# Cutting a weight load by partitions, and moving two cut points: attention decode with a parallel MLP on one core

## The chip, the core and the metric

The kernel runs on one core of one Trainium2 chip. A core has a matrix engine (PE), a vector engine (DVE), an activation engine (ACT), GpSimd (POOL) and a sync engine (SP), which here does nothing but issue transfers. Sixteen DMA engines move data between the memory outside the core (DRAM) and the on-chip memory (SBUF, 128 partitions). The metric is device time in microseconds (us) of one execution; lower is better. Before the change the median of three runs is 1283.76 us (1283.54 to 1283.78).

## The reference, cut to what matters

The batch is 8, with one query token of 640 values each. There are 32 heads of 128 values with 4096 cached keys and values, all in bfloat16. The block normalises x, runs attention over the caches and an MLP beside it, and adds both to x:

```
xn = layernorm(x)
q  = (xn @ wq), 32 heads of 128
o  = softmax(q k^T * 128^-0.5) v        # k, v: caches of 8 x 32 x 4096 x 128
out = x + o @ wo + (gelu(layernorm(xn) @ w1 + b1) @ w2 + b2)
```

The caches are 512 MB of the 552 MB that are read; wq and wo are 5.2 MB each, w1 and w2 2.2 MB each.

## The kernel before, in words

The work is cut into 32 items. Item i is one batch entry and one group of eight heads; its keys are one 8 MB load and its values another. A load fills one slot of the large tile `S_sb` with all 128 partitions: partition p holds 256 keys of one head (16 partitions for each head), 64 KB in one row. `S_sb` has three slots: two take the keys in turns, and the third takes the values, one item after another.

For each item, 176 of the 256 key columns are scored on DVE in three chunks (multiply, add, reduce), and 80 on PE and ACT (transposes, copies and small matmuls). Then come the maximum, the exponentials on ACT, and `pe_PV` (line 633): 256 matmuls, one for each key column, that accumulate the output of the item. The next value load may start only when `pe_PV` is done with the slot (`load_v`, line 362); the next key load waits until the item two before has been read (`load_k`, line 350).

Before the first item, the same slots hold the weights of the small stages: `wq_sb` and `w1_sb` lie in the value slot and `w2_sb` in a key slot. `wq_sb` has one row of 40 KB in each of 128 partitions (row p holds five of the 640 input rows). `w2` comes in two loads: `w2a` with 128 partitions, and `w2b`, the last 64 rows of w2, with 64 partitions. `pe_q` (line 448) waits for wq and makes all queries; `pe_mlp1` waits for w1, `pe_mlp2` for w2. The end of the MLP releases the second key slot and the value slot.

At the end, the key slot of item 30 takes wo in parts. `load_wl` brings two head groups and then one (`WL_CUT`), and `load_wn` brings the last group in three pieces (`WN_CUT`), each with a semaphore. `fin_wl` and `fin_wn` multiply them into the accumulator in the same order, and `fin_store` adds up and stores. The value load of the last item is cut into four pieces by key columns (`V_CUT`). The first of these may start when `pe_PV` of item 30 has gone through as many key columns as the piece has (the ticket `pvh`, set inside `pe_PV`); the other three wait for its end. `pe_PV` of the last item waits for each piece when it gets to its first column.

The order of work on each engine is written out by hand: `at(position, function, ...)` gives each step a place, the steps are sorted, and each engine replays its own list. All loads but the smallest are issued by SP, one after another, in this order: wq, w1, w2a, w2b, keys of item 0 in two pieces, and then keys and values by turns. The three small loads of x, b1 and b2 go out from ACT's queue.

Of the kernel before, what the change touches and what calls it, by code (L numbers as in the profile page):

```python
# [14 lines left out]
P = 128  # L15
# [176 lines left out]
def bass_parallel_sum__gqa_block_cached__mixer_channel_mlp__decode_kernel(  # L192
# [17 lines left out]
    HS = 8  # L210
# [4 lines left out]
    DC = D // P  # L215
# [7 lines left out]
    SLOT = NKEY * DH  # L223
    KA, KB, VS = 0, 1, 2
    WL_CUT = (0, 2, 3)
    WN_CUT = (0, 4, 7, HS)
    V_CUT = (0, 96, 176, 240, 256)
    K_CUT = (0, 117, 256)

    def jp_of(i):  # L230
# [17 lines left out]
    with ExitStack() as es:  # L248
# [3 lines left out]
        sem = lambda name: es.enter_context(nc.semaphore(name))  # L252
# [4 lines left out]
        def part(slot, lo, n, rows=P):  # L257
            return S_sb[0:rows, slot, lo:lo + n]

        wq_sb = part(VS, 0, DC * H * DH).rearrange("p (c n) -> p c n", c=DC)  # L260
# [6 lines left out]
        def scratch(n, rows=P):  # L267
# [60 lines left out]
        pe, dve, act, sp, pool = (_Eng(sem(f"{n}_s")) for n in ("pe", "dve", "act", "sp", "pool"))  # L328
        pe2, act2 = _Eng(sem("pe2_s")), _Eng(sem("act2_s"))
        ld_s = [_Dma(sem(f"ld_s{s}")) for s in range(3)]  # L330
        ld_x, ld_b1, ld_b2, ld_wq, ld_w1, ld_w2a, ld_w2b, st_o = (
            _Dma(sem(n)) for n in ("ld_x", "ld_b1", "ld_b2", "ld_wq", "ld_w1", "ld_w2a", "ld_w2b", "st_o"))
        ld_vl = [_Dma(sem(f"ld_vl{q}")) for q in range(1, len(V_CUT) - 1)]
        ld_k0 = _Dma(sem("ld_k0"))
        ld_wl = [_Dma(sem(f"ld_wl{q}")) for q in range(len(WL_CUT) - 1)]
        ld_wn = [_Dma(sem(f"ld_wn{q}")) for q in range(len(WN_CUT) - 1)]
        tk = {}
        prog = []

        def at(pos, fn, *a):  # L340
            prog.append((pos, len(prog), fn, a))
# [20 lines left out]
        def load_v(i):  # L362
# [4 lines left out]
            tk[("v", i)] = []  # L367
            for d, lo, hi in zip([ld_s[VS]] + ld_vl, V_CUT[:-1], V_CUT[1:]):
                if lo:
# [13 lines left out]
        def load_wn(q):  # L383
            lo, hi = WN_CUT[q], WN_CUT[q + 1]
            n = HS * DH
            tk[("wn", q)] = ld_wn[q].sig(sp.dma_start(
                woL_sb[:, NL, lo * D:hi * D],
                A_wo[NL * n:(NL + 1) * n, :].rearrange("(p s) n -> p (s n)", p=P)[:, lo * D:hi * D]))

        def consts_pool():  # L390
            pool.iota(iota_h, [[-HP, HS]], base=0, channel_multiplier=1)
            tk["iota"] = pool.sig(pool.iota(iota_i, [[1, P]], base=0, channel_multiplier=-1))
            for d, (ap, v) in zip([None] + ld_vl, (
                    (zeros_sb, 0.0), (ones_sb, 1.0), (mx_sb[:, :], 0.0), (mb_sb[:, :], 0.0))):
                inst = pool.memset(ap, v)
                if d is not None:
                    inst.call[3] = (d.sem, 1)
            tk["consts"] = pool.sig(pool.memset(ones_f[:, :], 1.0))
# [47 lines left out]
                xT_sb[:, w, :, :].rearrange("p c b -> p (c b)"), TR_ps[:, w, 0:DC * B])))  # L446

        def pe_q():
            pe.wait(tk["wq"], tk[("xT", 0)])
            CHB.use(pe)  # L450
            for h in range(H):
                for c in range(DC):
                    last = pe.matmul(QT_ps[:, h * B:(h + 1) * B], wq_sb[:, c, h * P:(h + 1) * P],
                                     xT_sb[:, 0, c, :], start=(c == 0), stop=(c == DC - 1))
            CHB.used(pe, pe.sig(last))
# [177 lines left out]
        def pe_PV(i):  # L633
            PVB.use(pe)
            pe.wait(tk[("exp", i)])
            for j in range(NKEY):
                if j == 0:
                    pe.wait(tk[("v", i)][0])
                elif j in V_CUT:
                    pe.wait_ge(ld_vl[V_CUT.index(j) - 1].sem, 1)  # L640
                last = pe.matmul(PV_ps[:, 0:HS], tile[VS][:, j, :], P_sb[:, :, j],
                                 start=(j == 0), stop=(j == NKEY - 1))
                if j == V_CUT[1] - 1:
                    tk[("pvh", i)] = pe2.sig(last)
# [86 lines left out]
        def fin_wn(q):  # L731
            lo, hi = WN_CUT[q], WN_CUT[q + 1]
            pe.wait(tk[("wn", q)], tk[("oS3", 0)], tk[("oS3", 1)])
            for r in range(lo, hi):
                for c in range(DC):
                    last = pe.matmul(ACC_ps[:, c * B:(c + 1) * B],
                                     woL_sb[:, NL, r * D + c * P:r * D + (c + 1) * P], oS3_sb[:, r, :],
                                     start=False, stop=(r == HS - 1), skip_group_check=True)
            if hi == HS:
                ACCB.used(pe, pe.sig(last))  # L740
# [16 lines left out]
        at(-900, load, "x", ld_x, x_sb, x2, act)  # L757
        at(-899, load, "b1", ld_b1, b1_sb, B_b1.rearrange("(o f) -> o f", o=1), act)
        at(-898, load, "b2", ld_b2, b2_sb, B_b2.rearrange("(o f) -> o f", o=1), act)
        at(-890, load, "wq", ld_wq, wq_sb, A_wq.rearrange("(p c) n -> p c n", c=DC))  # L760
        at(-880, load, "w1", ld_w1, w1_sb, B_w1.rearrange("(p c) f -> p c f", c=DC))
        at(-879, load, "w2a", ld_w2a, w2_sb[:, 0:FB, :], B_w2[0:FB * P, :].rearrange("(p c) n -> p c n", c=FB))
        at(-878, load, "w2b", ld_w2b, w2_sb[0:FLAST, FB, :], B_w2[FB * P:F, :])
        at(-870, load_k, 0)
        at(-800, consts_pool)
        at(-795, idents)
        at(NQ * Q - 1, sel_pool)
# [5 lines left out]
        at(-772, cp_xT, 1)  # L773
        at(-771, pe_acc0)
        at(-770, pe_q)
        at(-765, cp_q)
        at(-740, pe_mlp1)
# [35 lines left out]
        for q in range(len(WL_CUT) - 1):  # L813
            at(o - 55 if q == 0 else o + 50 + 0.1 * q, load_wl, q)
            at(o + 79.1 + 0.2 * q, fin_wl, q)
        for q in range(len(WN_CUT) - 1):
            at(o + 51 + q, load_wn, q)
# [80 lines left out]
```

## Time and profile before

The table is from one profiled execution.

| What | Value |
|---|---|
| median of three runs | 1283.76 us |
| profiled execution, its own time | 1283.81 us |
| its span, first to last instruction | 1281.8 us |
| moved by the main DMA queue | 551.79 MB, 11152 packets |
| mean rate over the span | 431 GB/s |
| busy share: DVE, PE, ACT, POOL | 85%, 52%, 37%, 7% |
| one item in the middle of the run | 38.7 us (7.0 us `pe_PV`, 31.6 us until the next values land) |
| wq: issue to landing | 15.7 us |
| pieces of the last group of wo: issue to landing | 21.6, 22.3 and 22.2 us |

To read it: the page cuts the span into 40 slices and gives for each the busy share of every engine in tenths, the mean share of the 16 DMA engines and the GB/s that they moved. Queries of the trace give the same for any stretch. In such a stretch a transfer's packet is counted where it starts, so a short stretch can show a share over 1; over a few microseconds it evens out. A packet here is one row of one partition, such as 64 KB for the caches and 40 KB for wq. The ratio of GB/s to share tells how fast the packets went that started there.

### The profile page before, as it was taken

The numbers are of one execution on the slowest core, as the hardware profiler recorded it, in microseconds if no ns is written. First come the engines' busy times: TensorE is split into PE (matmuls) and PEld (weight loads), VectorE is DVE, ScalarE is ACT, GpSimd is POOL, SyncE is SP. The second block draws the span as 40 slices with busy tenths as digits, with TensorE's granted clock in tenths as the row PEclk, the third lists the DMA queues.
The fourth block names the chain that finished last, engine by engine and source line by source line (L and its number), as shares of the span: only waits on it lengthen the run. The fifth ranks groups of instructions, "written<-read, shape, count | busy, mean of one in ns | idle before, by whom it ended". The sixth has DMA issues, their size and how long they took to land.

```text
span 1281.8 us, 34444 instructions
## 1 busy us (share of the span) xinstructions
PE 671.3 (52%) x13944; PEld 575.0 (45%) x13944; DVE 1095.1 (85%) x675; ACT 475.1 (37%) x904; POOL 88.7 (7%) x108
## 2 busy tenths in 40 slices
PE   4365554564544564544664644654545655545645
PEld 4254443453443553433553534543434544434545
DVE  1799988988888988888988888988889988889885
ACT  1344432344432344423344423344323344323441
POOL 0001000000000000000000000000000000000001
PEclk9955655566655656555655555565555555555555
DMA  9999999999999999999999999999999999999998
GB/s 396 436 439 424 442 427 438 427 442 427 436 429 442 427 436 429 442 427 434 432 442 427 434 432 440 429 434 432 440 430 432 432 442 429 432 432 442 429 417 369
DMA packets 11235, 551.99 MB, mean 431 GB/s; under 512 B 1292, under 2 KB 1493, under 8 KB 1878
## 3 DMA queue, kind: packets, MB, share of 16 engines
q1 hardware_dynamic: 11152, 551.79, 99.7%
q8 instruction: 9, 0.15, 0.0%
q10 hardware_dynamic: 70, 0.03, 0.0%
q14 instruction: 4, 0.03, 0.0%
HBM read 551.80 MB, written 0.01 MB: 430 GB/s over the span
## 4 chain that ended last, share of the span: by engine, by line
DMA 80%; PE 19%; ACT 1%; issue 1%; SPq 0%; another core or an unknown queue 0%; DVE 0%; POOL 0%; ACTq 0%
DMA S_sb<-in_A_v_cache_dram 74%; PE PV_ps L111 17%; DMA S_sb<-in_A_k_cache_dram 3%; DMA S_sb<-in_A_wo_dram 2%; DMA S_sb<-in_B_w_dram 2%; PE TR_ps L111 1%; PE CH_ps L111 1%; ACT P_sb L111 0%; PE ACC_ps L111 0%; SPq L111 0%; PE S_ps L111 0%; ACT KT_sb L111 0%; PE QB_ps L111 0%; ACT S_sb L111 0%
## 5 line engine op out<-in xcount | busy, mean ns | idle before, releaser
L111 PE MATMUL TR_ps<-ident_bf,S_sb 128*128 128x128 bf16 (+1 forms) x2570 | 341.5, 278 | 376.8 <-POOL kr_sb L111 366.0
L111 DVE TENSOR_TENSOR S_sb<-S_sb,qbc_sb 128x7552 bf16<-128x7552 bf16 (+1 forms) x96 | 388.8, 4050 | 136.8 <-DMA S_sb<-in_A_k_cache_dram 136.8
L111 PEld LDWEIGHTS TR_ps<-ident_bf,S_sb 128*128 (+2 forms) x2570 | 244.8, 103 | 434.6 <-issue 360.3
L111 DVE TENSOR_REDUCE Sd_sb<-S_sb 128x59 f32<-128x3776 bf16 (+1 forms) x96 | 390.2, 4065 | 6.0
L111 ACT ACTIVATE KT_sb<-TR_ps 128x1024 bf16<-128x1024 bf16 x320 | 326.9, 1023 | 125.6 <-PE TR_ps L111 115.5
L111 PE MATMUL PV_ps<-P_sb,S_sb 128*128 128x8 bf16 x8192 | 224.0, 175 | 149.3 <-DMA S_sb<-in_A_v_cache_dram 146.2
L111 PEld LDWEIGHTS PV_ps<-P_sb,S_sb 128*128 128x128 bf16 x8192 | 221.2, 103 | 152.2 <-DMA S_sb<-in_A_v_cache_dram 149.0
L111 ACT ACTIVATE P_sb<-Sd_sb,NB_sb 128x256 bf16<-128x256 f32 x256 | 126.2, 494 | 218.5 <-DVE NB_sb L111 218.5
L111 DVE TENSOR_TENSOR S_sb<-S_sb 128x3776 bf16<-128x3776 bf16 (+1 forms) x96 | 202.9, 2114 | 3.3
L111 ACT ACTIVATE oU_sb<-PV_ps 128x8 f32<-128x8 f32 x31 | 5.5, 177 | 393.2 <-PE PV_ps L111 393.2
L111 PE MATMUL S_ps<-qrep_sb,KT_sb 128*128 128x8 bf16 x2560 | 122.0, 177 | 35.5 <-ACT KT_sb L111 31.8
L111 PEld LDWEIGHTS S_ps<-qrep_sb,KT_sb 128*128 128x128 bf16 x2560 | 91.8, 103 | 66.6 <-ACT KT_sb L111 39.5
L111 POOL TENSOR_TENSOR oT_sb<-oU_sb,ri_sb 128x8 bf16<-128x8 f32 x31 | 68.2, 2199 | 389.4 <-DVE S_sb L111 366.1
L111 ACT ACTIVATION_READ_ACCUMULATOR P_sb<-Sd_sb,NB_sb 128x1 f32 x256 | 47.7, 186 | 0.0
L111 POOL COPY qrep_sb<-qT_sb 128x128 bf16<-128x128 bf16 x32 | 14.5, 453 | 455.6 <-PE S_ps L111 435.8
L111 DVE TENSOR_TENSOR S_ps<-S_ps,mask_sb 128x320 f32<-128x320 f32 (+2 forms) x67 | 32.7, 488 | 4.3 <-PE S_ps L111 4.3
L111 DVE TENSOR_REDUCE Sd_sb<-S_ps 128x40 f32<-128x320 f32 x64 | 31.5, 492 | 2.2
L111 POOL MEMSET kr_sb<- 128x1 f32 x32 | 3.1, 98 | 324.0 <-DMA S_sb<-in_A_k_cache_dram 324.0
L111 PE MATMUL CH_ps<-rs_sb,ones_f 128*128 128x8 f32 x64 | 17.3, 344 | 9.9 <-DVE oS_sb L111 6.2
L111 PE MATMUL QB_ps<-ident_bf,qrep_sb 128*128 128x128 bf16 x32 | 9.1, 285 | 22.6 <-DVE S_sb L111 21.5
L111 PEld LDWEIGHTS CH_ps<-rs_sb,ones_f 128*128 128x128 f32 x64 | 15.1, 292 | 10.1 <-DVE oS_sb L111 6.3
L111 ACT ACTIVATE qbc_sb<-QB_ps 128x128 bf16<-128x128 f32 x32 | 8.8, 276 | 27.8 <-PE QB_ps L111 27.8
(57 smaller groups left out, 119.1 us busy)
## 6 DMA issues: line engine op xcount, KB each, us to landing
S_sb<-in_A_wq_dram SPq DMA_DIRECT2D x1, 5120.0 KB, 15.7
S_sb<-in_A_k_cache_dram SPq DMA_DIRECT2D x1, 4448.0 KB, 43.2
S_sb<-in_A_k_cache_dram SPq DMA_DIRECT2D x1, 3744.0 KB, 33.3
S_sb<-in_A_v_cache_dram SPq DMA_DIRECT2D x1, 3072.0 KB, 10.7
S_sb<-in_A_wo_dram SPq DMA_DIRECT2D x1, 2560.0 KB, 31.2
S_sb<-in_A_v_cache_dram SPq DMA_DIRECT2D x1, 2560.0 KB, 12.5
S_sb<-in_B_w_dram SPq DMA_DIRECT2D x1, 2160.0 KB, 20.4
S_sb<-in_B_w_dram SPq DMA_DIRECT2D x1, 2080.0 KB, 25.3
```

The source lines that it names most:

```text
L111: inst = getattr(e, name)(*a, **k)
```

## The change

Three constants and what hangs on them are changed. wq is loaded by two transfers, the first with partitions 0 to 15 and the second with 16 to 127; both are issued where the one was, and `pe_q` waits for both. The first piece of the last value load has 80 key columns instead of 96, so `pvh` is given after 80 matmuls and the second piece has 96 columns instead of 80. The last group of wo comes in pieces of 5, 2 and 1 rows instead of 4, 3 and 1.

```diff
     WL_CUT = (0, 2, 3)
-    WN_CUT = (0, 4, 7, HS)
-    V_CUT = (0, 96, 176, 240, 256)
+    WN_CUT = (0, 5, 7, HS)
+    V_CUT = (0, 80, 176, 240, 256)
+    WQ_CUT = (0, 16, P)
...
+        ld_wqa = _Dma(sem("ld_wqa"))
...
-            for d, (ap, v) in zip([None] + ld_vl, (
+            for d, (ap, v) in zip([None] * (4 - len(ld_vl)) + ld_vl, (
...
         def pe_q():
-            pe.wait(tk["wq"], tk[("xT", 0)])
+            pe.wait(*[tk[("wq", lo)] for lo in WQ_CUT[:-1]], tk[("xT", 0)])
...
-        at(-890, load, "wq", ld_wq, wq_sb, A_wq.rearrange("(p c) n -> p c n", c=DC))
+        for d, lo, hi in zip((ld_wqa, ld_wq), WQ_CUT[:-1], WQ_CUT[1:]):
+            at(-890 + lo / P, load, ("wq", lo), d, wq_sb[lo:hi],
+               A_wq.rearrange("(p c) n -> p c n", c=DC)[lo:hi])
```

The line with `zip` gives the same list as before, since `V_CUT` still makes four pieces. The instructions on PE, DVE, ACT and POOL stay the same in kind and number; SP has one transfer more.

## The prediction

> **What bounds the kernel now.** I read the page's slices first, then the chain that ended last, then the DMA issues, and at last short stretches of the trace at the places that the change touches.
>
> ```profile
> DMA  9999999999999999999999999999999999999998
> GB/s 396 436 439 424 442 427 438 427 442 427 436 429 442 427 436 429 442 427 434 432 442 427 434 432 440 429 434 432 440 430 432 432 442 429 432 432 442 429 417 369
> ...
> DMA 80%; PE 19%; ACT 1%; issue 1%; SPq 0%; another core or an unknown queue 0%; DVE 0%; POOL 0%; ACTq 0%
> ```
>
> The DMA engines are 90% busy or more in every slice but the last, at 424 to 442 GB/s in all but the first and the last two. The chain that ended last is made of value loads and of the `pe_PV` that frees their slot:
>
> ```profile
> 1215.30 31.62 DMA S_sb<-in_A_v_cache_dram
> 1246.97 7.01 PE PV_ps L111 x256
> ...
> 1256.27 22.26 DMA S_sb<-in_A_wo_dram
> 1278.57 0.71 PE ACC_ps L111 x20
> ```
>
> The reader should see that the 7.01 us of PE are not time without transfers. A value load of 8.39 MB takes 19.4 us at 433 GB/s, yet lands 31.6 us after its issue: some 12 us of other work lie ahead of it in the queue. So the kernel is one stream of transfers, and what is lost anywhere in it comes back as time at the end. 551.79 MB at 433 GB/s take 1274 us; 1.75 us before the first packet, 3.3 us after the last landing, and some 2.7 us of small losses make up the span of 1281.8.
>
> The start, in stretches (us; then busy time and instructions by engine; the last three columns are PE clock, DMA share, GB/s):
>
> ```profile
> 1.60:2.20 0.60, 0.00 (x0) 0.00 (x0) 0.39 (x4) 0.24 (x1) 0.02 (x1) 1.00 3.70 1041
> 2.20:3.20 1.00, 0.00 (x0) 0.00 (x0) 0.80 (x2) 1.00 (x1) 0.00 (x0) 1.00 0.00 0
> 3.20:3.80 0.60, 0.00 (x0) 0.00 (x0) 0.41 (x3) 0.13 (x2) 0.00 (x0) 1.00 0.23 68
> ...
> 23.50:24.50 1.00, 1.00 (x14) 0.93 (x14) 0.00 (x0) 0.00 (x0) 0.00 (x0) 1.00 1.01 433
> 24.50:25.40 0.90, 0.90 (x12) 0.83 (x11) 0.00 (x0) 0.00 (x0) 0.00 (x0) 1.00 1.73 622
> 25.40:26.10 0.70, 0.70 (x10) 0.67 (x10) 0.00 (x0) 0.00 (x0) 0.00 (x0) 1.00 0.26 92
> 26.10:26.90 0.80, 0.80 (x12) 0.75 (x11) 0.00 (x0) 0.00 (x0) 0.00 (x0) 1.00 1.54 612
> 27.30:28.10 0.80, 0.80 (x11) 0.73 (x10) 0.00 (x0) 0.00 (x0) 0.00 (x0) 1.00 1.39 599
> ```
>
> 1041 GB/s over 0.6 us are 625 KB, 15 rows of 40 KB: fifteen DMA engines start between 1.6 and 2.2 us. 68 GB/s over 0.6 us are one row more: the sixteenth starts at 3.2 or later. The other rows are the only load before that does not write all 128 partitions: `w2b`, 80 KB in 64 partitions, started around 24.5 to 26. Packets ahead of it and behind it move 429 to 431 GB/s for each full share (433/1.01, 599/1.39). In 24.5:25.4 the ratio is 360, in 25.4:26.1 354, in 26.1:26.9 397.
>
> **wq in 16 and 112 partitions.** This takes away one issue of 0.38 us on SP and adds two like it. w1, w2 and the keys of item 0 are thus issued about 0.45 us later (wq's issue starts at 0.73, w1's at 1.18), behind data that fill the engines until 16 us and more: free. Item 1's keys wait for the MLP, done at 31.75, while the 18.05 MB issued before keep the engines busy until about 43.5: 12 us of cover, and 10 to 20 us of delay in wq would move both alike. `pe_q` waits for one semaphore more, and behind it on PE wait the MLP's matmuls; all of that sits in the same cover.
>
> What counts is the stream. A first transfer of one row for each engine might start all engines at once. At most the sixteenth gains 1.5 us and the others about 0.2; the engines share the work and each had small delays later, so I take -0.2 (0 to -1.5).
>
> Against it stands how fast rows land that go to few partitions. Busy time beyond 430 GB/s in the three stretches: 1.73 x 0.9 - 560/430 = 0.25; 0.26 x 0.7 - 64/430 = 0.03; 1.54 x 0.8 - 490/430 = 0.09; together 0.37 us, charged to a load whose 82 KB should take 0.19. So a load to 64 partitions held up the stream by about twice its own time. wq's first 16 rows are 655 KB, 1.52 us of stream. If 16 partitions crowd no more than 64, they add 2 x 1.52 = 3.0 us. If time goes with the inverse of the partitions written, 8 times, they add 7 x 1.52 = 10.7 us. The row lies nearer to the first end in kind, but 16 is a quarter of 64; I take the geometric middle, +5.7. The other side, no crowding at all, is the first rival.
>
> [...]
>
> The 112 partitions are seven rows for each engine, 4.59 MB, 10.7 us of stream. The 128-partition rows go at full rate: 0. At the ratio of the 64-partition load they would add 21 us, and on a straight line between 128 and 64, a quarter of that, 5.3. The nearest row is 128, so I take 1.5 (0 to 5.3; I give 21 no weight).
>
> **First piece of the last V.** 256 matmuls in 7.01 us are 27 ns each, so `pvh` comes 16 x 27 = 0.44 us earlier and the first piece is issued at 1249.3 instead of 1249.73.
>
> ```profile
> 1250.25:1251.25 1.00, 1.00 (x44) 1.00 (x41) 1.00 (x1) 0.00 (x0) 0.00 (x0) 0.50 0.99 414
> 1251.25:1251.50 0.25, 0.25 (x16) 0.25 (x13) 0.25 (x1) 0.00 (x0) 0.00 (x0) 0.50 1.67 582
> 1251.50:1252.00 0.50, 0.50 (x25) 0.50 (x22) 0.50 (x1) 0.00 (x0) 0.00 (x0) 0.50 0.77 324
> 1252.00:1252.50 0.50, 0.50 (x25) 0.50 (x23) 0.50 (x1) 0.00 (x0) 0.00 (x0) 0.50 1.32 533
> ```
>
> Where that piece takes over from wo's first part the GB/s for a full share drop to 349 (582/1.67): a few engines ran dry or waited. An earlier issue can win at most its 0.44 us for these; I take -0.2. The second piece then has 96 columns but ends at the same column 176 and the same byte. It is needed at column 80, 1266.87 + 80 x 0.027 = 1269.05, and landed 12.5 us after its issue at 1254.0, at 1266.5: 2.5 us of margin, and a late stream would move both. No cost.
>
> **Pieces of wo's last group.** The first piece lands one row later, 164 KB or 0.38 us: from 1277.4 (1255.79 + 21.6) to 1277.8. Its 25 matmuls at 27 ns end at 1278.45, before the second piece, whose last byte has not moved (1278.53). Behind that wait 10 matmuls instead of 15 stand ahead of the last 5: up to 5 x 27 ns = 0.13 us. I take -0.1 (-0.13 to +0.1). Nothing is issued more or less often.
>
> **The sum.** Against the profiled execution, 1283.81 (span 1281.8 and 2.0 around it, 0.05 above the median of the runs shown): -0.2 (start) + 5.7 (16 rows) + 1.5 (112 rows) - 0.2 (V) - 0.1 (wo) = 1290.5.
>
> **The rivals.**
> 1. *No crowding.* The slow rows at 24.5 to 26.9 come from small packets (1280 bytes) or from a new source, and 16 rows of 40 KB land as fast as ever. For it: only 0.37 us speak against it, and wq's very first rows, to all 128 partitions, are slow as well (281 GB/s for a full share, 1041/3.70, in 1.60:2.20). Against it: the start of w1, w2a and item 0's second piece shows no such drop, and rows of 64 KB beside it keep their rate. Sum: 1283.81 - 0.2 - 0.2 - 0.1 = 1283.3, not slower. It turns into the forecast when the two pieces of wq lose more than about 3 us.
> 2. *The delay is absorbed.* wq lands late, but a later hole in the stream takes it up: 1283.5 or so. Against it: no slice but the last is below 0.9, and the queue holds 12 us of work at each value issue.
> 3. *The 112 rows crowd too.* 10.7 for the first piece or 5.3 for the second, or both: 1294 to 1300. For it: in seven rows for each engine an even share of partitions can't be kept; against it: the 128-row loads show no trace of crowding.
> 4. *The start gains in full.* The late sixteenth engine is what ends last: -1.5, -0.44 and -0.13 give 1281.7, still within 0.2%.
>
> **How the numbers follow.** 0.2% of the time, 2.6 us, is about what a measurement of this kernel can tell from no change: 1281.2 to 1286.3. Forecast, crowding in the first piece mainly, 1286.3 to 1294: 0.43. Rival 3: 0.14. Rival 1: 0.34. Rival 2: 0.04. Rival 4: 0.05. Time 1290.5 by the likeliest, whose own range is 1286.3 to 1294. The range reaches down to rival 1, with 0.5 for its terms, 1282.8, and up into rival 3 to 1295.5; left out are most of rival 4 and half of rival 3 and little else. Slower: 0.43 + 0.13 = 0.56; faster: 0.02, out of rival 4 with more gains than I can name; within: 0.42.
>
> **What would show it.** If right: PE's first matmul of the queries moves from 16.46 to 22 or later; after 2.2 us the stretches show few bytes for some 4 to 10 us; from about 30 us all is the same but later, with 38.7 us for each item; the wait for wo at the end is unchanged within 0.2 us. If rival 1 holds, the query matmuls start at 16.5 or before and the slices equal those of before. I am wrong if that first matmul comes early, or if it comes late and the last value load does not.

## The result and the profile after

The changed kernel takes 1296.13 us (median of six runs, 1295.91 to 1296.18) against 1283.76 us before: a ratio of 1.0096, 95% interval [1.0083, 1.0109]. It is 12.4 us slower. The prediction named the side, and the range ended at 1295.5, 0.6 us too low.

The profiled execution has a span of 1294.2 us. The page's slices after, with their GB/s, and the shares of the chain that ended last (both follow the same rows of before in the prediction):

```profile
DMA  9999999999999999999999999999999999999998
GB/s 244 435 433 433 427 435 435 427 440 429 440 433 427 435 435 427 438 431 440 431 429 435 435 427 438 431 440 431 430 435 433 431 433 433 440 429 433 433 418 362
...
DMA 80%; PE 19%; issue 1%; ACT 0%; SPq 0%; another core or an unknown queue 0%; DVE 0%; POOL 0%; ACTq 0%
```

Only the first slice differs by more than 15 GB/s: 244 instead of 396. Over its 32 us that is 4.9 MB less, 11 us of stream at 433 GB/s. The row of busy shares says nothing of it: its first slice shows a 9 in both kernels, at 396 GB/s before and at 244 after. Rate must be read beside share.

The first microseconds in stretches (us; busy time and instructions of each engine; then PE clock, DMA share, GB/s), first before the change and then after it:

```profile
0.00:2.20 2.20, 0.00 (x0) 0.00 (x0) 0.81 (x5) 0.24 (x1) 0.99 (x11) 1.00 1.01 284
2.20:4.00 1.80, 0.00 (x0) 0.00 (x0) 1.27 (x5) 1.25 (x2) 0.00 (x0) 1.00 0.19 68
4.00:6.00 2.00, 0.36 (x5) 0.27 (x5) 1.49 (x5) 0.00 (x0) 0.00 (x0) 1.00 1.24 534
```

```profile
0.00:2.20 2.20, 0.00 (x0) 0.00 (x0) 0.81 (x5) 0.24 (x1) 0.99 (x11) 1.00 1.57 209
2.20:4.00 1.80, 0.00 (x0) 0.00 (x0) 0.31 (x1) 1.04 (x1) 0.00 (x0) 1.00 0.88 114
4.00:6.00 2.00, 0.08 (x2) 0.08 (x3) 1.49 (x6) 0.20 (x1) 0.00 (x0) 1.00 0.00 0
6.00:8.00 2.00, 0.28 (x5) 0.19 (x5) 1.35 (x6) 0.20 (x1) 0.00 (x0) 1.00 1.79 328
8.00:10.00 2.00, 0.36 (x5) 0.27 (x5) 0.72 (x3) 0.00 (x0) 0.00 (x0) 1.00 0.00 0
10.00:12.00 2.00, 0.00 (x0) 0.00 (x0) 0.00 (x0) 0.00 (x0) 0.00 (x0) 1.00 1.42 329
...
26.00:28.00 2.00, 0.00 (x0) 0.00 (x0) 0.00 (x0) 0.00 (x0) 0.00 (x0) 1.00 0.87 320
28.00:30.00 2.00, 1.66 (x63) 1.70 (x64) 0.00 (x0) 0.00 (x0) 0.00 (x0) 1.00 0.99 423
```

After the change, the bytes that start in the first 4 us (209 x 2.2 + 114 x 1.8 = 665 KB) are the sixteen rows of the first piece, and no packet starts between 4 and 6 us: all sixteen engines are still in their first row of 40 KB. GB/s for a full share is 183 at 6 us (328/1.79), 232 at 10 us, and 427 from 28 us on, when w1 with its 128 partitions is under way. The wq transfers in the list of DMA issues, KB and us to landing:

```profile
S_sb<-in_A_wq_dram SPq DMA_DIRECT2D x1, 4480.0 KB, 27.0
...
S_sb<-in_A_wq_dram SPq DMA_DIRECT2D x1, 640.0 KB, 8.7
```

Before, all 5120 KB landed in 15.7 us. Now the 640 KB alone take 8.7. The query matmuls start when wq is there (timeline, start and duration; before, then after):

```profile
16.46 4.43 PE L111 MATMUL CH_ps<-S_sb 128*128 128x8 bf16 x160 [4.89 <-DMA S_sb<-in_A_wq_dram]
```

```profile
28.34 4.41 PE L111 MATMUL CH_ps<-S_sb 128*128 128x8 bf16 x160 [9.21 <-DMA S_sb<-in_A_wq_dram]
```

That is 11.88 us later. In the chain of waits, item 1's keys are issued 11.80 us later, and nothing of it is won back (before, then after):

```profile
31.75 34.55 DMA S_sb<-in_A_k_cache_dram
905.69 31.64 DMA S_sb<-in_A_v_cache_dram
...
1278.57 0.71 PE ACC_ps L111 x20
```

```profile
43.55 34.56 DMA S_sb<-in_A_k_cache_dram
918.03 31.64 DMA S_sb<-in_A_v_cache_dram
...
1290.13 1.49 PE ACC_ps L111 x40
```

The value load that starts at 918.03 stood at 905.69 before: 12.34 us. The last accumulation ends at 1291.62 instead of 1279.28: 12.34 again. The step from 11.80 to 12.34 lies in the profile before, not in the change. Three kernels below that load wq whole start the query matmuls at 15.89 or 15.90 and issue item 1's keys at 31.18 or 31.19, and yet have the value load at 905.60 to 905.71, as before. One of them:

```profile
15.90 4.43 PE L111 MATMUL CH_ps<-S_sb 128*128 128x8 bf16 x160 [4.29 <-DMA S_sb<-in_A_wq_dram]
...
31.19 0.33 SPq L111 DMA_DIRECT2D S_sb<-in_A_k_cache_dram  x1
```

So the profiled execution of before happened to be half a microsecond late in its query stage, which cost it nothing. Against these three the key load after the change is 12.4 us late (43.55 - 31.19): the whole loss is there by the end of the MLP, and nothing is added afterwards.

### The profile page after: what moved, and what is told of

It is laid out like the page before. It is cut to its first block, busy times and chain, and to the rows that moved or that the text cites. A ratio compares the mean times of both kernels' runs of the same rounds, so it can differ in the third digit from the quotient of the medians.

```text
span 1294.2 us, 34446 instructions
## 1 busy us (share of the span) xinstructions
PE 669.9 (52%) x13944; PEld 575.0 (44%) x13944; DVE 1095.1 (85%) x675; ACT 475.0 (37%) x904; POOL 84.0 (6%) x108
## 4 chain that ended last, share of the span: by engine, by line
DMA 80%; PE 19%; issue 1%; ACT 0%; SPq 0%; another core or an unknown queue 0%; DVE 0%; POOL 0%; ACTq 0%
DMA S_sb<-in_A_v_cache_dram 73%; PE PV_ps L111 17%; DMA S_sb<-in_A_k_cache_dram 3%; DMA S_sb<-in_B_w_dram 2%; DMA S_sb<-in_A_wo_dram 2%; PE TR_ps L111 1%; PE CH_ps L111 1%; ACT P_sb L111 0%; PE ACC_ps L111 0%; PE S_ps L111 0%; SPq L111 0%; ACT KT_sb L111 0%; PE QB_ps L111 0%; ACT S_sb L111 0%
## 5 line engine op out<-in xcount | busy, mean ns | idle before, releaser
L111 POOL TENSOR_TENSOR oT_sb<-oU_sb,ri_sb 128x8 bf16<-128x8 f32 x31 | 64.0, 2065 | 390.7 <-DVE S_sb L111 353.9
## 6 DMA issues: line engine op xcount, KB each, us to landing
S_sb<-in_A_v_cache_dram SPq DMA_DIRECT2D x1, 3072.0 KB, 12.5
```

The costliest lines, as they stand in the source:

```text
L111: inst = getattr(e, name)(*a, **k)
```

## The experiments

The theory to test: rows written to a part of the partitions slow each other down ("crowd"), so the cut of wq is the whole loss. Its rivals: the other two edits take part, a second transfer at a cold start costs by itself, or the number of rows counts and not their place. The "ways in" of some expectations are a picture of mine: no run shows them, only which partitions are slow.

### wq's cut alone

```diff
-    V_CUT = (0, 80, 176, 240, 256)
-    WN_CUT = (0, 5, 7, HS)
+    V_CUT = (0, 96, 176, 240, 256)
+    WN_CUT = (0, 4, 7, HS)
     WQ_CUT = (0, 16, P)
```

(against the changed kernel)

> The kernel before with wq's load alone cut into 16 and 112 partitions. [...] In the trace after the change the first query matmul comes 11.9 us later (28.34 against 16.46), so this kernel is 11.5 to 12 us slower than before, with the query matmuls at 28.3. Rival, the end counts too: the last wait after the change was for the first piece of wo, with 40 matmuls behind it instead of 20, so some 0.5 us of the 12.4 are not in this kernel. Rival, the three edits disturb one another: clearly less than 11 us.

Measured: 1296.26 us, ratio 1.0094 [1.0079, 1.0110]. The query matmuls start at 28.80:

```profile
28.80 4.41 PE L111 MATMUL CH_ps<-S_sb 128*128 128x8 bf16 x160 [9.79 <-DMA S_sb<-in_A_wq_dram]
```

All of the loss is in this cut, 12.5 us against 12.4, and half a microsecond more than the 11.5 to 12 expected; the part that I had put down to wo is not missing here.

### The last value load alone, wo's pieces alone, and both together

```diff
-    V_CUT = (0, 96, 176, 240, 256)
+    V_CUT = (0, 80, 176, 240, 256)
```

(against the kernel before)

> The kernel before with the first piece of the last value load at 80 columns instead of 96, nothing else. Theory: the piece is issued 0.44 us earlier; the queue still holds wo's first part, so the gain is between 0 and 0.44 us (1283.3 to 1283.8), below what a measurement tells. Rival, the second piece of 96 columns comes late: the matmuls of the last item pause at column 80, and the time rises by up to 1 us.

```diff
-    WN_CUT = (0, 4, 7, HS)
+    WN_CUT = (0, 5, 7, HS)
```

(against the kernel before)

> The kernel before with wo's last group in pieces of 5, 2 and 1 rows, nothing else. My forecast had -0.1 us here. The trace after the change says otherwise: the first piece is the last thing waited for, and all 40 matmuls (1.49 us) follow it, where before 20 (0.71 us) followed the second piece. By that this kernel is 0.3 to 0.7 us slower, 1284.1 to 1284.5. By the forecast it is 1283.7 and 15 matmuls follow the last wait.

```diff
-    WQ_CUT = (0, 16, P)
+    WQ_CUT = (0, P)
...
-        for d, lo, hi in zip((ld_wqa, ld_wq), WQ_CUT[:-1], WQ_CUT[1:]):
+        for d, lo, hi in zip((ld_wq,), WQ_CUT[:-1], WQ_CUT[1:]):
```

(against the changed kernel, with one load of wq again)

> The changed kernel with wq's cut alone undone: one load to 128 partitions again, the last value load at 80 columns and wo in 5, 2 and 1 rows as changed. Theory: the whole loss is in wq; 1283.5 to 1284.1, the same as before. Rival, the three edits disturb one another: more than 1284.5.

Measured: 1283.74 us, 1.0000 [0.9991, 1.0009], for the value load; 1283.76 us, 0.9999 [0.9990, 1.0008], for wo; 1283.81 us, 1.0001 [0.9991, 1.0010], for both. No gain and no loss that can be told. The chain of the kernel with wo's pieces alone shows why both my readings of it missed:

```profile
1255.84 21.89 DMA S_sb<-in_A_wo_dram
1277.73 0.04 issue
1277.78 1.51 PE ACC_ps L111 x40
```

The last wait that delayed a matmul has moved from the second piece (1278.53) to the first (1277.73), and 40 matmuls follow instead of 20. But they run from 1277.78 to 1279.29, and before the change 20 ran from 1278.57 to 1279.28: the same end. A count of matmuls behind the last wait is no price when the wait itself comes earlier. The forecast had let 25 matmuls at 27 ns, the pace of `pe_PV`, end before the second piece lands. These 40 take 1.51 us, 38 ns each on average; at that pace, an estimate, the 25 end near 1278.7, after the second piece has landed, so PE doesn't wait for it.

### wq cut by columns

```diff
-    WQ_CUT = (0, 16, P)
+    WQ_CUT = (0, 1, DC)
...
-            at(-890 + lo / P, load, ("wq", lo), d, wq_sb[lo:hi],
-               A_wq.rearrange("(p c) n -> p c n", c=DC)[lo:hi])
+            at(-890 + lo / P, load, ("wq", lo), d, wq_sb[:, lo:hi, :],
+               A_wq.rearrange("(p c) n -> p c n", c=DC)[:, lo:hi, :])
```

(against the kernel with wq's cut alone)

> The kernel before with wq's load cut into two as well, but by columns: the first transfer brings one fifth of every row (8 KB), the second four fifths, both to all 128 partitions. Theory, crowding: a cut that leaves all partitions in each transfer costs nothing; 1283.4 to 1284.2, queries at 16.2 to 16.7. Rival, a second transfer at the cold start costs by itself (its descriptors, its semaphore, the small first piece): 3 us or more slower, like the change.

Measured: 1283.63 us, 0.9999 [0.9990, 1.0008]. Two transfers, a small one first, at the same cold start, cost nothing here, where each writes all 128 partitions. The query matmuls start at 15.50. Kernels with the whole load and nothing added have them anywhere from 15.89 to 16.46, so little of this is the cut's doing, and the time does not move.

### The order turned round, and two halves

```diff
-    WQ_CUT = (0, 16, P)
+    WQ_CUT = (0, 112, P)
```

(this one and the next against the kernel with wq's cut alone)

> The kernel before with wq's load cut the other way round: 112 partitions first, then the last 16. Theory, crowding: both pieces still suffer whatever their order; in the trace of the 16 and 112 cut the stream lost about 3.5 us on the first row of each DMA engine and about 8.3 us on the seven rows after it, so this kernel is 7 to 12 us slower than before, and the query matmuls start between 23 and 28.5. Rival, cold start: the 16 rows cost only because they were the first transfer, when the engines had nothing else; then this kernel is less than 3 us slower, or loses only what 112 rows lose by themselves.

```diff
-    WQ_CUT = (0, 16, P)
+    WQ_CUT = (0, 64, P)
```

> The kernel before with wq cut into 64 and 64 partitions. Theory, crowding by place: each half reaches only a part of the ways in, and does so for its whole length; if the price per byte is that of the 64-row load of w2 in the kernel before (0.37 us lost on 0.19 us of bytes), 10 us and more are lost, up to 21. [...] Rival, it is the unequal size of the pieces or the 16 rows that cost: clearly less than the 16 and 112 cut, under 6 us.

Measured: 1295.49 us, 1.0092 [1.0075, 1.0109], with 112 first; 1297.23 us, 1.0104 [1.0088, 1.0121], with two halves. With 112 rows first the loss is 11.8 us: the 16 rows are not slow because they come first. Two halves lose 13.5 us, no less than the others, so it is not the small piece either. Of the expectations, the theory's held in both.

### The same bytes to chosen partitions

These kernels leave wq whole and add a transfer of wq's rows to a part of a key slot that nothing reads. The computation is unchanged; the time has the added bytes in it. The edits, against the kernel before, differ in the first two lines shown (a semaphore for the transfer is not shown):

```diff
+        ext_sb = scratch(4 * H * DH)
...
+        at(-885, load, "ext", ld_e, ext_sb[0:16], A_wq.rearrange("(p c) n -> p (c n)", c=DC)[0:16, 0:4 * H * DH])
...
-            pe.wait(tk["h"], tk["w2a"], tk["w2b"])
+            pe.wait(tk["h"], tk["w2a"], tk["w2b"], tk["ext"])
```

with `ext_sb[0:P:8]` for the rows spread out, and all of `ext_sb` for the controls.

> The kernel before with one transfer more: 16 rows of 32 KB of wq (524 KB) to partitions 0 to 15 of an unused part of a key slot, issued right behind wq's whole load, in a running stream. The bytes themselves are 1.2 us of stream at 430 GB/s. Theory, crowding by place: partitions 0 to 15 share few ways in, and the row that cost 3.5 us too much with 40 KB costs 2.8 us with 32 KB; 3.5 to 5 us slower than before. [...] Rival, cold start: only the 1.2 us of its bytes.

> As the run with 16 extra rows at partitions 0 to 15, but the same 16 rows go to partitions 0, 8, 16 and so on to 120. Bytes, number of rows and rows for each DMA engine are the same. Theory, crowding by place: it depends on which partitions are written, so the rows spread out cost clearly less than those at 0 to 15, 2 to 3 us against 3.5 to 5. [...] Rival, crowding by number: what counts is that there are only 16 rows, or one for each DMA engine; then both cost the same.

> Control for the two runs with 16 extra rows: the same 524 KB in 128 rows of 4 KB to all 128 partitions, at the same place in the order. Both theories: 1.1 to 1.4 us slower than before, the time of the bytes. If it costs as much as the 16 rows, the extra transfer itself is what costs, and neither theory holds.

> The kernel before with an extra transfer of 112 rows of 36 KB (4.13 MB) to partitions 0 to 111 of an unused part of a key slot, behind wq. The bytes are 9.6 us of stream at 430 GB/s. Theory: 112 rows, seven for each DMA engine, crowd by themselves; from the 16 and 112 cut, less what 16 rows cost in a running stream (3.8 us lost for 32 KB rows, 4.8 for 40 KB), 112 rows lose 7 to 7.7 us of 10.7, so here 6.3 to 7 beyond the bytes: 15.5 to 17 us slower than before. Rival: only 16 rows crowd, and the 112 merely had to wait for them: 9.6 to 11 us.

> Control for the run with 112 extra rows: the same 4.13 MB in 128 rows of 31.5 KB to all partitions. Both theories: the time of the bytes, 9.4 to 9.9 us slower than before.

After these, it was open why 112 rows, which leave out only an eighth of the partitions, ran at about half rate (231 GB/s against 434 for 128 rows). Three more kernels asked whether a transfer is slow because it does not reach some part of the range, or because of the way its rows are dealt out to the engines (`ext_sb[0:64]`, `ext_sb[0:P:2]`, `ext_sb[0:96]`).

> The kernel before with an extra transfer of 64 rows of 36 KB (2.36 MB) to partitions 0 to 63, behind wq. The bytes are 5.5 us at 430 GB/s; at the 204 GB/s that wq in 64 and 64 partitions showed, 11.6 us. Both theories say 10.5 to 12 us slower than before; it is the partner of the run with every second partition.

> The same 64 rows to every second partition, 0, 2, 4 and so on to 126. Theory, reach: a transfer is slow because it leaves out a part of the partition range; these rows leave out none, so 5.5 to 7 us. Theory, dealing out: with fewer than 128 rows neighbouring rows go to one engine, and two engines then write into the same part at the same time, wherever the rows lie; so as slow as at 0 to 63, 10 to 12 us. The 16 rows spread out lost 2.1 us against 3.8, between the two.

> The kernel before with an extra transfer of 96 rows of 36 KB (3.54 MB) to partitions 0 to 95, behind wq; the bytes are 8.2 us at 430 GB/s. Theory, dealing out: any number of rows but 128 runs at about half rate; 14 to 17.5 us slower than before. Theory, reach: the rate goes with the part of the range that is written, three quarters, so 10 to 12 us.

All eight are in the table. The rate is the added bytes by the difference of the medians, to the kernel before of the same comparison; "lost" is what goes beyond the bytes at the 434 GB/s of the large control.

| Partitions of the added transfer | MB | us slower | ratio, 95% interval | GB/s | lost us |
|---|---|---|---|---|---|
| all 128 | 0.52 | 1.23 | 1.0010 [1.0000, 1.0019] | 426 | 0.0 |
| 0 to 15 | 0.52 | 5.04 | 1.0042 [1.0028, 1.0056] | 104 | 3.8 |
| 0, 8, ... 120 | 0.52 | 3.34 | 1.0025 [1.0015, 1.0036] | 157 | 2.1 |
| all 128 | 4.13 | 9.52 | 1.0075 [1.0058, 1.0092] | 434 | 0.0 |
| 0 to 63 | 2.36 | 12.07 | 1.0093 [1.0076, 1.0110] | 195 | 6.6 |
| 0, 2, ... 126 | 2.36 | 5.71 | 1.0047 [1.0030, 1.0064] | 413 | 0.3 |
| 0 to 95 | 3.54 | 16.91 | 1.0135 [1.0118, 1.0152] | 209 | 8.8 |
| 0 to 111 | 4.13 | 17.90 | 1.0138 [1.0121, 1.0155] | 231 | 8.4 |

The intervals are 2.4 to 4.4 us wide, so the last digits of the rates mean little: the 104 could be anything from 73 to 146, and two of that kernel's five executions took a microsecond longer than the others. The intervals of the two kernels with 16 rows overlap. Their first stretch of the added transfer tells them apart; partitions 0 to 15 are in the first fence, every eighth partition in the second:

```profile
14.30:15.30 1.00, 0.00 (x0) 0.00 (x0) 0.00 (x0) 0.00 (x0) 0.00 (x0) 1.00 3.45 492
14.30:17.30 3.00, 0.00 (x0) 0.00 (x0) 0.00 (x0) 0.00 (x0) 0.00 (x0) 1.00 1.22 175
```

```profile
14.30:15.30 1.00, 0.00 (x0) 0.00 (x0) 0.00 (x0) 0.00 (x0) 0.00 (x0) 1.00 1.96 492
14.30:17.30 3.00, 0.03 (x1) 0.04 (x2) 0.00 (x0) 0.00 (x0) 0.00 (x0) 1.00 1.01 244
```

The same 492 GB/s start, fifteen rows of 32 KB, but the rows at 0 to 15 take 3.45 us of all sixteen engines, those spread out 1.96; at 434 GB/s it would be 1.13. For 64 rows, first those at 0 to 63, then those on every second partition:

```profile
14.30:17.30 3.00, 0.41 (x15) 0.41 (x16) 0.00 (x0) 0.00 (x0) 0.00 (x0) 1.00 1.31 295
17.30:20.30 3.00, 3.00 (x119) 3.00 (x117) 0.00 (x0) 0.00 (x0) 0.00 (x0) 1.00 1.02 209
```

```profile
14.30:17.30 3.00, 0.84 (x31) 0.85 (x32) 0.00 (x0) 0.00 (x0) 0.00 (x0) 1.00 0.98 419
17.30:20.30 3.00, 3.00 (x119) 3.00 (x116) 0.00 (x0) 0.00 (x0) 0.00 (x0) 1.00 1.00 421
```

205 against 421 GB/s for a full share (209/1.02, 421/1.00), with the same bytes, the same rows of DRAM and the same place in the order of loads. The partitions that are written decide, and that is shown; the intervals of the two times don't overlap. And the 112 rows, followed by their control of 128 rows in the same stretch:

```profile
17.30:20.30 3.00, 3.00 (x118) 3.00 (x116) 0.00 (x0) 0.00 (x0) 0.00 (x0) 1.00 1.07 246
```

```profile
17.30:20.30 3.00, 3.00 (x115) 2.95 (x111) 0.00 (x0) 0.00 (x0) 0.00 (x0) 1.00 0.90 387
```

230 against 430 (246/1.07, 387/0.90). So the 112 rows crowd by themselves; they did not merely wait for the 16. Three expectations were a little too low: 15.5 to 17 us for the 112 rows (17.90 measured), 2 to 3 for the 16 rows spread out (3.34), and at most 12 for 64 rows at the start (12.07).

What follows for the theories. "Cold start" and "number of rows" have fallen. The "dealing out" theory said that 64 rows on every second partition would be as slow as 64 at the start: 5.71 us against 12.07, so it is wrong in that form. The "reach" theory was right there, but gave 10 to 12 us for 96 rows: they took 16.91. Partitions 0 to 95 and 0 to 111 leave out only a quarter and an eighth of the range and still run at about half rate, 209 and 231 GB/s against 434. What may be left is a mixture of the two theories, which I only argue: no run shows which partitions are written at the same time. How 96 and 112 rows are dealt to the engines is not in the views of the trace. So that a piece of 64, 96 or 112 consecutive partitions runs at about half rate is measured (195, 209 and 231 GB/s, with 434 for all 128); why it does stays open.

## Why the prediction came out as it did

*The stream is the bound, and what it loses at the start comes back at the end.* Right. The first key load that waits is 11.8 to 12.4 us late, the end 12.34, with items of 38.70 us in between. Rival 2, a hole that takes up the delay, is out: half a microsecond was taken up in the profile before, but 12 are not. The sign named for this, a late first query matmul and a late last value load, came.

*The start, -0.2.* The start itself came as hoped: all sixteen rows had begun by 3.2 us, where before the sixteenth began at 3.2 or later. But those rows then took so long that a gain can't be told from the loss, and no run shows this term by itself.

*Sixteen rows, +5.7 between 3.0 and 10.7.* Right in kind, too high in size: as a transfer by itself they lost 3.8 us for rows of 32 KB, by size 4.8 for wq's 40 KB, and in the changed kernel less than that (below). The 0.37 us behind the 64-row load of w2 pointed the right way, but no run separates crowding there from its packets of 1280 bytes. Their ratio, two for one, was too high for 64 rows: wq in two halves lost 13.5 us on 12.2 of bytes (5.24 MB at 430 GB/s), 1.1 for one, and too low for 16 rows: 3.8 on 1.2, or 3.2 for one.

*112 rows, +1.5.* This is the step that failed: "The nearest row is 128, so I take 1.5 (0 to 5.3; I give 21 no weight)." I drew a straight line from 64 to 128 partitions and went below even that, and there is no such line. 64, 96 and 112 rows from the first partition run at 195, 209 and 231 GB/s, 128 rows at 434: nearly all of the gain comes between 112 and 128, where no run was made. 112 rows of 36 KB lost 8.4 us; by size that is 9.3 for wq's. (These went to partitions 0 to 111, the change's to 16 to 127.) At 1.1 for one, the ratio that wq's two halves measured, the term would have been 11.8.

With these prices the sum is 1283.8 + 4.8 + 9.3 = 1297.9, 1.8 us above the 1296.13. The stretches of the changed kernel give both terms directly. Up to 4 us the sixteen rows keep the engines busy for 1.57 x 2.2 + 0.88 x 1.8 = 5.04 us of a full share; 665 KB at 433 GB/s take 1.54, so 3.5 are lost. Before, the rows that start in the same 4 us are slow as well: 2.56 us for 747 KB, which take 1.73. That is 0.8 lost already, so the 16 rows add 2.7. From 4 to 26 us, added up in stretches of 2 us, the share comes to 19.6 us for 4.73 MB (the 112 rows and the first few of w1), which take 10.9: 8.7 are lost. So where the prediction had 5.7 (3.0 to 10.7) and 1.5 (0 to 5.3), the changed kernel shows 2.7 and 8.7, together 11.4 of the 12.4 us; the last microsecond I have not placed. The two errors pull in opposite ways, and by that luck the time of the sum was nearer than its terms.

*The last value load, -0.2, and wo, -0.1.* Nothing: 1.0000 [0.9991, 1.0009] and 0.9999 [0.9990, 1.0008]. In wo the new first piece does become the last that is waited for, and the forecast, which priced these matmuls at the pace of others, said it would not. The end does not move.

*The rivals.* Rival 3, with both pieces crowding, 1294 to 1300 and a chance of 0.14, is what happened, though it gave the larger price, 10.7, to the first piece and 5.3 to the second, and it was the second that cost more (2.7 and 8.7). Its reason, that seven rows for each engine can't keep an even share of partitions, no run shows. Rival 1, no crowding, had 0.34, in good part since one slow stretch of 0.37 us seemed thin; there is crowding, 12 us of it.

## What to carry to other kernels

If a kernel is one stream of transfers, give every large load all 128 partitions, and if it must be cut, cut it by columns: here a cut into ranges of consecutive partitions brought the first piece down to 132 GB/s for a full share (665 KB in 5.04 us, where 747 KB had taken 2.56) and the second to 241 (4.73 MB in 19.6 us, against 433), and 640 KB moved by themselves cost 12 us for the whole; the cut by columns cost nothing (0.9999 [0.9990, 1.0008]). Look for the first load in the kernel that writes fewer partitions, compare GB/s for a full share around it with its neighbours', and test a drop by a run even if it is short. The busy shares of the DMA engines didn't show it here: a 9 at 396 GB/s and at 244.

## What the runs showed that I had not expected

112 of 128 partitions run at 231 GB/s, little over half of the 434 for 128, while 64 rows on every second partition run at 413. Sixteen rows spread over the range gained only a part (157 GB/s against 104). And in kernels that all took 1283.6 to 1283.8 us the query stage starts anywhere from 15.50 to 16.46: so much earlier or later is worth nothing where it isn't the stream that moves.
